# Attention with a long convolution on one core: the fill moves to 64x32 tiles, two results at a time, and PV of a new accumulator comes two turns late

## The chip, the cores and the metric

The kernel runs on one core of one Trainium2 chip. The metric is the device time of one execution in microseconds (us). Engines: PE is TensorE, DVE is VectorE, ACT is ScalarE, POOL is GpSimd, SP is SyncE.

## The reference

Two independent parts, put side by side in the last dimension of the output (2048 x 1024, f32). Part A is attention with 32 heads of 16 and one shared K and V; part B is a short and a long causal convolution with gates. Cut to what is computed:

```python
# A: x (1,2048,512), H = 32, Dh = 16
q = heads(x @ wq); k = x @ wk; v = x @ wv
p = softmax(einsum("bhqd,bkd->bhqk", q, k) * Dh**-0.5)
a = concat_heads(einsum("bhqk,bkd->bhqd", p, v)) @ wo
# B: q, k, v (1,2048,512)
k_shift = sum(k_pad[:, t:t+S, :] * shift_k[:, 3-t] for t in range(4))
kv = k_shift * v
y = irfft(rfft(kv, 4096) * rfft(ssm_k, 4096))[:, :2048] + kv * ssm_D
b = q * y
return concatenate([a, b], -1)
```

## The kernel before, in words

**The attention** (attend, L816) goes over 1024 tiles. A tile is one chunk of 128 keys (of 16) against 256 queries of each of four heads; 16 tiles share an accumulator, and two such groups make one of the 32 stacks n. For tile t, scores (L769) issues eight matmuls (S, L779), f16, 49 rows by 32 columns of PE, 512 columns wide: row half e of PE writes bank e of a two-bank tile s, of which there are two. One exponential on ACT (L787) reads both banks and writes p; seven p tiles rotate. pv (L790) issues eight f32 matmuls (P, L799; each runs as two passes, so the profile counts 16), 64 rows by 32 columns, 256 wide: row half e adds into the accumulator bank acc[e]. After 16 tiles DVE copies one accumulator and adds the other (L811, L812) and, but for the last two stacks, SP stores the sum to DRAM (L814).

The program uses eight banks of PSUM: four for s, and four (pool pf, L102, given out by bank) shared by the two accumulators and everything else on PE.

**Everything else is fill**, written as generators that yield before each piece of work: rest_of_q (L710: q of the other heads, then bounds for the exponent, L634), conv_pe (L432: transposes of the long kernel at L305; forward products with a table of cosines at L250 with a copy at L255; backward products at L397 with a multiplication by q at L426), conv_short and conv_dve (the element-wise work of the convolution on DVE), wo_heads and wo_part (L897: normalisation, then the output projection). Products run as mm (L200): four matmuls of 128 rows by 32 columns, side by side in column strips, so each product uses all 128 rows. f16 products are cut into hi and lo parts (three, L219). columns (L205) and products (L223) issue them in pieces: one result in one bank at a time, and a unit is 512 f16 or 128 f32 columns of one product.

**The order** is made ahead by _Fill (L983), as if two budgets ran along with the tiles. Every second tile, turn (L1018) adds RATE (L49) to them: 1.8 units of PE work and 1700 ns of DVE work, capped by MOST; threads other than the hurried one and conv_pe get at most EASY = 2 units. step (L1022) asks the threads in turn. A thread that has begun a result is the holder until it has finished it, and nobody else begins one. A yield of WAIT, n puts the thread off by n steps of two tiles. In attend the scores of tile x + 2 come first, then fill that goes on, P of tile x, and fill that is new; at the first tile of a group fill stands ahead of P. hurry (L703) lets q go first within LEAD steps of its need.

A prologue loads, transposes x and makes the first q; last (L957) ends the attention and the projection. The program has a second path for inputs of unusual size (_general), which is not taken here.

Of the kernel before, what the change touches and what calls it, by code (L numbers as in the profile page):

```python
# [48 lines left out]
RATE = 1.8, 1700.0  # L49
EASY = 2  # L50
MOST = 3.0, 2900.0
# [5 lines left out]
LEAD = 32  # L57
# [35 lines left out]
WHOLE, PARTS = 0, 1  # L93


class _Emit:
    def __init__(self, ctx, tc, I, out):
        self.ctx, self.tc, self.nc, self.I, self.out = ctx, tc, tc.nc, I, out
        e = ctx.enter_context
        self.c = e(tc.tile_pool(name="c", bufs=1))  # L100
        self.ps = e(tc.tile_pool(name="ps", bufs=2, space=PSUM))
        self.pf = e(tc.tile_pool(name="pf", bufs=4, space=PSUM))  # L102
        self.w = e(tc.tile_pool(name="w", bufs=2))
        self.dr = e(tc.tile_pool(name="dr", bufs=1, space=DRAM))
        self.n = 0
        self.step = 0
        self.seen = set()
# [97 lines left out]
    def columns(self, bank, first, w, x, last=False, dve=0):  # L205

        n, k = 0, x.shape[-1] // P
        while n < k:  # L210
            g = yield k - n, dve, CONT if bank else NEW, PARTS
            start = not bank
            if start:
                bank.append(self.bank())
            c = slice(P * n, P * (n + g))
            n += g
            self.mm(bank[0][:, P * first + c.start : P * first + c.stop], w, x[:, c], start, last and n == k)

    def three(self, w, x):  # L219

        return [(w[:, i], x[:, j]) for i, j in ((0, 0), (1, 0), (0, 1))]

    def products(self, bank, pairs, last=False, dve=0):  # L223

        n, k = 0, len(pairs)
        while n < k:
            g = yield k - n, dve, CONT if bank else NEW, PARTS
            start = not bank
            if start:
                bank.append(self.bank())  # L230
            for w, x in pairs[n : n + g]:
                n += 1
                self.mm(bank[0], w, x, start, last and n == k)
                start = False
# [15 lines left out]
    def forward(self, src, c, m, ft):  # L250

        b = []
        for q in range(2):
            yield from self.columns(b, 2 * q, ft[:, q, :], src, q == 1, 700 * q)
        self.nc.vector.tensor_copy(c[:, :, m, :], b[0].rearrange("p (q n) -> p q n", q=2))  # L255
# [9 lines left out]
    def conv_load(self):  # L265
# [3 lines left out]
        sk = self.w.tile([P, 4, 4], F32, tag="gn", bufs=2, name="sk")  # L269
        nc.sync.dma_start(sk, I["B_shift_k"].rearrange("(c p) t -> p c t", p=P))  # L270
        yield WAIT, 6
        yield 1, 600, NEW, WHOLE
# [19 lines left out]
    def long_forward(self, blk, hin, ch):  # L292
# [16 lines left out]
        for m in (0, 2):  # L309
            yield 2, 700, NEW, WHOLE  # L310
            turn(m)
        for m in range(0, 16, 2):
            if m < 12:
                ft[m // 2 + 2] = self.table("ff", m // 2 + 2)
                yield 2, 700, NEW, WHOLE
                turn(m + 4)
            for i in range(2):
                yield from self.forward(hT[m][:, i, :], ch, m + i, ft[m // 2][:, i])
# [51 lines left out]
    def short_forward(self, blk, cx):  # L370

        ft = {i: self.table("ff", i) for i in range(2)}
        for m2 in range(8):
# [3 lines left out]
            for i in range(2):  # L377
                yield from self.forward(self.kv2[m2][:, i, :], cx, 2 * m2 + i, ft[m2][:, i])
# [18 lines left out]
    def backward(self, blk, cx, places):  # L397
# [15 lines left out]
        for m2 in range(8):  # L413
# [5 lines left out]
            b = []  # L419
            for i in range(2):  # L420
                m = 2 * m2 + i
                for cc in range(2):
                    x = cx[:, cc, 4 * g2[m // 4] + g1[m % 4], :]
                    last = i == cc == 1
                    yield from self.columns(b, 2 * i, ft[m2][:, i, cc, :], x, last, 700 * last)
            nc.vector.tensor_tensor(r, b[0].rearrange("p (i n) -> p i n", i=2), q[m2], ALU.mult)  # L426
# [61 lines left out]
    def load(self):  # L488
# [4 lines left out]
        wkv = w.tile([P, 4, 32], F32, tag="gn", bufs=2, name="wkvf")  # L493
# [79 lines left out]
    def k_rows(self, c, cut):  # L573

        nc = self.nc
        h16 = self.w.tile([P, 512], F16, tag="gn", bufs=2, name=self.nm("kh"))
# [34 lines left out]
    def q_mm(self, g, c, b, dk):  # L611
        for i, (w, x) in enumerate(self.three(self.wq[g][:, :, dk, :], self.xT[c][:, :, dk, :])):
            self.mm(b, w, x, start=dk == i == 0, stop=dk == 3 and i == 2)

    def q_out(self, g, c, b, spread=False):
# [5 lines left out]
        qa = w.tile([P, 512], BF16, tag="qa", bufs=1, name=self.nm("qa"))  # L621
# [12 lines left out]
    def bound(self, g, c, b, st=None):  # L634
# [4 lines left out]
        gn = w.tile([8, 512], F16, tag="gn", bufs=2, name=self.nm("gn"))  # L639
# [70 lines left out]
    def rest_of_q(self):  # L710
# [5 lines left out]
        for c in range(4):  # L716
            for g in range(4):
                self.qn = c, g
                if c == g == 0:
                    continue  # L720
                if c or g > 1:
                    b = []
                    for dk in range(4):
                        pairs = self.three(self.wq[g][:, :, dk, :], self.xT[c][:, :, dk, :])
                        yield from self.products(b, pairs, dk == 3, 2600 * (dk == 3))
                    self.q_out(g, c, b[0])
                yield WAIT, 2
                yield 2, 1100, NEW, WHOLE
                self.bound(g, c, self.bank())
                self.qs.add((g, c))  # L730
# [20 lines left out]
    def flag(self):  # L751
# [10 lines left out]
        yield 1, 200, NEW, WHOLE  # L762
# [5 lines left out]

    def scores(self, u):  # L769


        n, (h, k) = u // (2 * NKT), divmod(u % (2 * NKT), NKT)
        if n >= NQ:
            return
# [15 lines left out]
    def pv(self, x):  # L790

        nc, w = self.nc, self.w
        n, (h, k) = x // (2 * NKT), divmod(x % (2 * NKT), NKT)
        if k == 0:
            self.acc = [self.bank() for _ in range(2)]
# [10 lines left out]
        if k < NKT - 1:  # L806
            return
        if h == 0:
            self.ao = w.tile([P, 512], F32, tag="ao", bufs=1, name=self.nm("ao"))
        cols = slice(256 * h, 256 * h + 256)  # L810
        nc.vector.tensor_copy(self.ao[:, cols], self.acc[0][:, 0:256])  # L811
        nc.vector.tensor_tensor(self.ao[:, cols], self.ao[:, cols], self.acc[1][:, 0:256], ALU.add)  # L812
        if n < NQ - 2:
            nc.sync.dma_start(self.od[n, :, cols], self.ao[:, cols])  # L814

    def attend(self, fill):  # L816
        self.od = self.dr.tile([NQ, P, 512], F32, name="od")
        tiles = 2 * NQ * NKT
        for x in range(tiles - 2):
# [66 lines left out]
    def wo_rows(self, i, groups):  # L886

        b = []
        for G in groups:
            yield from self.wo_row(b, i, G, G == groups[-1])  # L890
        return b[0]

    def wo_row(self, b, i, G, last):
        pairs = self.three(self.oc[G][:, :, i * P : (i + 1) * P], self.wo[G % 4])
        yield from self.products(b, pairs, last, 700 * last)

    def wo_part(self):  # L897
        nc, w, I = self.nc, self.w, self.I
        xr = self.out.rearrange("b (c p i) d -> (b c) p i d", c=4, p=P, i=4)
        for c in range(3):  # L900
            yield from self.after(("oc", 4 * c + 3))
            for i in range(4):
                b = yield from self.wo_rows(i, range(4 * c, 4 * c + 4))
                t = self.s2("wp", (512,))
                nc.vector.tensor_scalar(t, b, 1 / (OS * WS), None, ALU.mult)
                nc.sync.dma_start(xr[c][:, i, 0:D], t)
# [4 lines left out]
        for i in range(4):  # L911
            b = yield from self.wo_rows(i, range(12, 14))
            nc.vector.tensor_scalar(self.wp[i], b, 1 / (OS * WS), None, ALU.mult)
# [10 lines left out]
        for i in range(4):  # L924
            b = []
            yield from self.wo_row(b, i, 14, True)
            nc.vector.scalar_tensor_tensor(self.wp[i], b[0], 1 / (OS * WS), self.wp[i], ALU.mult, ALU.add)
        both = w.tile([P, 2, 4, 512], F32, tag="in", bufs=1, name="lr")
        t, self.lr = both[:, 0], both[:, 1]
        for h in range(2):  # L930
            while self.step < NKT * (NQ - 1) + 1 - NKT // 2 * (1 - h):
                yield WAIT, 1
            yield 0, 1800
            self.over(self.ao[:, 256 * h : 256 * h + 256], t, h)
        for i in range(4):
            b = []
            yield from self.columns(b, 0, t[:, 2, i * P : (i + 1) * P], self.wl[0], True, 700)
            nc.vector.tensor_tensor(self.wp[i], self.wp[i], b[0], ALU.add)
        while self.step < NKT * (NQ - 1) + NKT // 2 + 1:
# [43 lines left out]
class _Fill:  # L983
# [3 lines left out]
    def __init__(self, threads, hurry):  # L987
# [3 lines left out]
        self.used = 0  # L991
        self.holder = None

# [7 lines left out]
    def ask(self, t, i):  # L1001

        while t[0] is not None and t[2] <= i:
            if t[1] is None:
                self.go(t, None)
            elif t[1][0] == WAIT:
                t[2] = i + t[1][1]
# [5 lines left out]
    def give(self, t, n):  # L1013
# [4 lines left out]
    def turn(self):  # L1018
        self.used = 0
        self.credit = [min(c + r, m) for c, r, m in zip(self.credit, RATE, MOST)]  # L1020

    def step(self, i, new):  # L1022

        c, once = self.credit, True
        used = self.used
        more = True
        while more:
            more = False
            first = self.hurry()
            for t in sorted(self.threads, key=lambda t: t is not self.threads[first or 0]):  # L1030
# [4 lines left out]
                if a[0] > 0:  # L1035
                    most = int(c[0])
                    if t is not self.threads[1] and t is not self.threads[first or 0]:
                        most = min(most, EASY - used)
                    n = a[0] if a[3] == WHOLE else min(a[0], most)
                    if n < 1 or n > most or not (once and new or self.holder is t) or self.holder not in (None, t):  # L1040
                        continue
                    once = False
                elif c[1] <= 0 or not new:
# [4 lines left out]
                self.give(t, n)  # L1048
                more = True
                break  # L1050
        self.used = used
# [161 lines left out]
```

## Time and profile before

| what | value |
|---|---|
| median of 3 runs | 1091.48 us (1091.24 to 1093.11) |
| the profiled execution's own time | 1091.16 us |
| its span, first to last instruction | 1089.4 us |
| PE busy | 96% of the span |
| ACT busy | 91% |
| DVE busy | 63% |
| POOL busy | 10% |
| DMA queues q1 and q0, share of 16 engines | 12.6% and 11.6% |
| granted TensorE clock | 0.995 |

How to read it: a group's row names line, engine, operation, output <- input and shape, then busy time, mean ns of one, and the idle time of the engine just before, with what ended it. "128*32" or "64*32" behind a matmul is the part of PE that it uses, rows by columns. PEld is the weight load, which may overlap the matmuls. Matmuls are pipelined, so their starts say more than their ends. A row of the timeline gives start, length and count of merged instructions, in us from the start of the span.

### The profile page before, as it was taken

The numbers are of one execution on the slowest core, as the hardware profiler recorded it, in microseconds if no ns is written. First come the engines' busy times: TensorE is split into PE (matmuls) and PEld (weight loads), VectorE is DVE, ScalarE is ACT, GpSimd is POOL, SyncE is SP. The second block draws the span as 40 slices with busy tenths as digits, with TensorE's granted clock in tenths as the row PEclk, the third lists the DMA queues.
The fourth block names the chain that finished last, engine by engine and source line by source line (L and its number), as shares of the span: only waits on it lengthen the run. The fifth ranks groups of instructions, "written<-read, shape, count | busy, mean of one in ns | idle before, by whom it ended". The sixth has DMA issues, their size and how long they took to land.

```text
span 1089.4 us, 61326 instructions
## 1 busy us (share of the span) xinstructions
PE 1046.7 (96%) x28603; PEld 510.3 (47%) x28603; DVE 683.9 (63%) x978; ACT 988.3 (91%) x1038; POOL 105.3 (10%) x158
## 2 busy tenths in 40 slices
PE   6899999999999999999999999999999999999996
PEld 4344444445444444544454444444444445554432
DVE  3748676885178888884886467698889832121132
ACT  3699999999999999999999989999999999999974
POOL 3232101000000000013021311000000001210000
PEclk9999999999999999999999999999999999999999
DMA  7354614111322112114133532011131013221101
GB/s 232 114 149 163 197 50 145 52 51 49 113 70 86 31 35 64 55 59 137 40 116 100 177 108 99 30 46 45 60 98 51 30 35 109 87 79 31 36 3 43
DMA packets 51984, 89.18 MB, mean 82 GB/s; under 512 B 11612, under 2 KB 34186, under 8 KB 50700
## 3 DMA queue, kind: packets, MB, share of 16 engines
q1 hardware_dynamic: 38316, 43.50, 12.6%
q0 software_dynamic: 11648, 40.89, 11.6%
q8 instruction: 225, 3.69, 1.4%
q10 hardware_dynamic: 1760, 0.81, 0.3%
q14 instruction: 35, 0.29, 0.1%
HBM read 60.16 MB, written 25.02 MB: 78 GB/s over the span
## 4 chain that ended last, share of the span: by engine, by line
PE 76%; ACT 15%; issue 4%; DVE 3%; DMA 1%; ACTq 0%; SPq 0%; DVEq 0%
PE f L799 37%; PE s L779 19%; PE f L203 18%; ACT p L787 15%; PE f L305 1%; DVE xT L540 1%; DMA wqf<-in_A_wq 1%; PE f L638 0%; PE x L528 0%; ACT xT L539 0%; DMA qd<-gn 0%; PE x L203 0%; DVE t L362 0%; DVE ao L811 0%; DVE sp L255 0%
## 5 line engine op out<-in xcount | busy, mean ns | idle before, releaser
L787 ACT ACTIVATE p<-s 128x1024 f32<-128x1024 f32 x1024 | 976.6, 1039 | 70.4 <-PE s L779 41.2
L799 PE MATMUL f<-p,vx 64*32 64x256 f32 x16384 | 667.6, 381 | 3.6 <-DVE ao L811 2.0
L779 PE MATMUL s<-st,kst 49*32 49x512 f16 x8192 | 436.0, 381 | 14.4 <-issue 4.3
L799 PEld LDWEIGHTS f<-p,vx 64*32 64x32 f32 x16384 | 277.0, 106 | 182.8 <-issue 99.6
L779 PEld LDWEIGHTS <-kst 49*32 49x32 f16 x8192 | 164.9, 90 | 177.2 <-issue 114.4
L141 DVE TENSOR_TENSOR sp<-sp 128x1024 f32<-128x1024 f32 x96 | 111.7, 1212 | 0.0
L255 DVE COPY sp<-f 128x512 f32<-128x512 f32 x64 | 44.1, 689 | 89.5 <-PE f L203 89.3
L811 DVE COPY ao<-f 128x256 f32<-128x256 f32 x64 | 27.0, 421 | 99.9 <-PE f L799 99.8
L203 PE MATMUL f<-xT,wq 128*32 128x512 f16 x768 | 61.8, 395 | 0.0
L203 PE MATMUL f<-wo,o 128*32 128x512 f16 x720 | 59.1, 385 | 0.7 <-issue 0.7
L141 DVE TENSOR_TENSOR sp<-sp,sp 128x1024 f32<-128x1024 f32 x48 | 56.6, 1217 | 0.3
L203 PE MATMUL f<-a,ff 128*32 128x128 f32 (+1 forms) x792 | 45.4, 314 | 0.4 <-issue 0.4
L259 POOL DMA_DIRECT2D ff<-in_ff x32 | 17.5, 549 | 288.0 <-PE f L203 288.0
L203 PE MATMUL f<-sp,fi 128*32 128x128 f32 (+1 forms) x784 | 43.6, 315 | 0.0
L203 PE MATMUL f<-hT,ff 128*32 128x256 f32 (+1 forms) x632 | 42.8, 350 | 0.0
L426 DVE TENSOR_TENSOR r<-f,q 128x512 f32<-128x512 f32 x16 | 11.0, 690 | 48.6 <-PE f L203 48.6
L427 POOL DMA_DIRECT2D out<-r x16 | 11.4, 714 | 238.7 <-DVE r L426 224.7
L364 DVE TENSOR_TENSOR a<-a,t 128x512 f32<-128x512 f32 x48 | 33.1, 690 | 1.3
L362 DVE TENSOR_TENSOR t<-kk,tpb 128x512 f32<-128x512 f32 x48 | 32.8, 683 | 0.0
L203 PEld LDWEIGHTS <-wq 128*32 128x32 f16 x768 | 14.2, 96 | 39.6 <-issue 38.2
L203 PEld LDWEIGHTS f<-a,ff 128*32 128x32 f32 x792 | 16.8, 108 | 33.0 <-issue 28.8
L812 DVE TENSOR_TENSOR ao<-ao,f 128x256 f32<-128x256 f32 x64 | 27.0, 421 | 7.7 <-DVE ao L811 0.9
(136 smaller groups left out, 576.8 us busy)
## 6 DMA issues: line engine op xcount, KB each, us to landing
ff<-in_ff POOLq DMA_DIRECT2D x32, 256.0 KB, 4.7
od<-ao SPq DMA_DIRECT2D x60, 128.0 KB
kk<-in_B_k POOLq DMA_DIRECT2D x12, 640.0 KB, 5.4
qd<-qp SPq DMA_DIRECT2D x48, 128.0 KB
st<-qd SPq DMA_DIRECT2D x60, 98.0 KB
v<-in_B_v POOLq DMA_DIRECT2D x16, 256.0 KB, 5.9
hin<-in_B_ssm_k POOLq DMA_DIRECT2D x4, 1024.0 KB, 6.8
fi<-in_fi POOLq DMA_DIRECT2D x16, 256.0 KB, 3.9
```

The source lines that it names most:

```text
L141: v.tensor_tensor(part(out), part(a), part(b), op)
L203: self.nc.tensor.matmul(out[j : j + 32], w[:, j : j + 32], x, start=start, stop=stop)
L255: self.nc.vector.tensor_copy(c[:, :, m, :], b[0].rearrange("p (q n) -> p q n", q=2))
L259: self.nc.gpsimd.dma_start(t, self.I[n][:, 2 * m2 : 2 * m2 + 2])
L362: nc.vector.tensor_tensor(t, kx(i), tap(i), ALU.mult)
L364: nc.vector.tensor_tensor(a, a, t, ALU.add)
L427: nc.gpsimd.dma_start(self.orr[:, 2 * m2 : 2 * m2 + 2, D + blk * CB : D + (blk + 1) * CB], r)
L779: self.nc.tensor.matmul(s[j : j + 32, e, :], self.kst[rows, k * P + j : k * P + j + 32], self.st[n][rows, :, 256 * h : 256 * h + 256], sta ...
L787: self.nc.scalar.activation(p, s, AF.Exp, scale=DH**-0.5 / SC / SC)
L799: nc.tensor.matmul(self.acc[e][32 * j : 32 * j + 32, 0:256], self.vx[rows, k, :], self.pt[x][rows, j % 2, 256 * (j // 2) : 256 * (j // 2) ...
L811: nc.vector.tensor_copy(self.ao[:, cols], self.acc[0][:, 0:256])
L812: nc.vector.tensor_tensor(self.ao[:, cols], self.ao[:, cols], self.acc[1][:, 0:256], ALU.add)
```

## The change

- Fill is issued by halves, which takes two results a and b of the same number of products and two banks. In the first half, row half 0 of PE works for a in bank 0 and row half 1 for b in bank 1, each on its own 64 rows of the contraction; then the thread waits (WAIT 1.5), and in the second half the row halves change places: row half 0 now adds to b's bank and row half 1 to a's. Each matmul has 64 rows by 32 columns. forward, backward, rest_of_q and wo_part now make two results at a time; backward's multiplication is split by result. Transposes and bounds stay as they were.
- _Fill has one call per tile, after P: 1.15 units and 850 ns per tile, at most EASY = 2 units a tile for all threads, caps 4 units and 1700 ns. WAIT counts tiles, twice the number given. After a result is done, no thread begins another for GAP = 2 tiles. LEAD is 44.
- plan puts P of tiles 0 and 1 of a group at tile 2's turn and P of tiles 2 and 3 at tile 3's.
- qa shares the buffers "gn", of which there are three instead of two; ao of the last stack uses buffer "r".

```diff
-RATE = 1.8, 1700.0
+RATE = 1.15, 850.0
 EASY = 2
-MOST = 3.0, 2900.0
+MOST = 4.0, 1700.0
-LEAD = 32
+LEAD = 44
+GAP = 2
...
+    def halves(self, a, b, grain, dve=0):
+        banks = []
+        for half in range(2):
+            n, k = 0, len(a)
+            while n < k:
+                g = yield (k - n) * grain, dve * half, CONT if banks else NEW, grain
+                start = not banks
+                if start:
+                    banks += [self.bank(), self.bank()]
+                for m in range(n, n + g // grain):
+                    for e in range(2):
+                        out, (cols, w, x) = banks[half ^ e], (a, b)[half ^ e][m]
+                        r = slice(64 * e, 64 * e + 64)
+                        for j in range(0, P, 32):
+                            self.nc.tensor.matmul(
+                                out[j : j + 32, cols],
+                                w[r, j : j + 32],
+                                x[r],
+                                start=half == m == 0,
+                                stop=half == 1 and m == k - 1,
+                            )
+                n += g // grain
+            if half == 0:
+                yield WAIT, 1.5, CONT
+        return banks
...
     def forward(self, src, c, m, ft):
-        b = []
-        for q in range(2):
-            yield from self.columns(b, 2 * q, ft[:, q, :], src, q == 1, 700 * q)
-        self.nc.vector.tensor_copy(c[:, :, m, :], b[0].rearrange("p (q n) -> p q n", q=2))
+        work = [[(slice(CB * q, CB * q + CB), ft[:, i, q, :], src[:, i, :]) for q in range(2)] for i in range(2)]
+        b = yield from self.halves(*work, 2, 1400)
+        for i in range(2):
+            self.nc.vector.tensor_copy(c[:, :, m + i, :], b[i].rearrange("p (q n) -> p q n", q=2))
...
+            b = yield from self.halves(*work, 2, 850)
+            for i in range(2):
+                nc.vector.tensor_tensor(r[:, i, :], b[i][:, cols], q[m2][:, i, :], ALU.mult)
...
+                    b = yield from self.halves(*work, 1, 5200)
+                    for i in range(2):
+                        self.q_out(g + i, c, b[i])
...
+    def plan(self):
+        plan = {}
+        for x in range(2 * NQ * NKT):
+            plan.setdefault(x + {0: 2, 1: 1, 2: 1}.get(x % NKT, 0), []).append(x)
+        return plan
...
             self.scores(t)
-            self.step = x // 2
-            if x % 2 == 0:
-                fill.turn()
-            if x % NKT == 0:
-                fill.step(self.step, True)
-                self.pv(x)
-            elif x % 2:
-                self.pv(x)
-            else:
-                fill.step(self.step, False)
-                self.pv(x)
-                fill.step(self.step, True)
+            self.step, self.slot = x // 2, x
+            for y in plan.get(x, []):
+                self.pv(y)
+            fill.turn(x)
...
             if self.holder is None:
+                self.free = i + GAP
...
+                    most = min(int(c[0]), EASY - used)
+                    n = min(a[0], most) // a[3] * a[3]
+                    if n < 1 or self.holder not in (None, t) or (self.holder is None and i < self.free):
                         continue
```

More of the change, by code (lines that the diff above doesn't have):

```diff
@@ L203, in mm @@
             self.nc.tensor.matmul(out[j : j + 32], w[:, j : j + 32], x, start=start, stop=stop)
[L205 to L217, printed above, removed]
[L219 to L234 removed]
+    def halves(self, a, b, grain, dve=0):
[23 more added lines that the diff above has]
+        return banks
+    def three(self, w, x):
+        return [(slice(0, 512), w[:, i], x[:, j]) for i, j in ((0, 0), (1, 0), (0, 1))]
     def parts(self, engine, hi, lo, x, scale):
@@ L884, in wo_heads, with wo_rows @@
             self.seen.add(("oc", G))
[L886 to L895, printed above, removed]
+    def wo_rows(self, i, groups, dve):
+        work = [
+            [y for G in groups for y in self.three(self.oc[G][:, :, r * P : (r + 1) * P], self.wo[G % 4])] for r in (i, i + 1)
+        ]
+        return (yield from self.halves(*work, 1, dve))
     def wo_part(self):
```

159 lines of the change are left out of this document (77 added, 82 removed).

## The prediction

> **What bounds the kernel now.** I read the page first: who is busy, and what the chain that ended last is made of.
>
> ```profile
> PE 1046.7 (96%) x28603; PEld 510.3 (47%) x28603; DVE 683.9 (63%) x978; ACT 988.3 (91%) x1038; POOL 105.3 (10%) x158
> ...
> PE 76%; ACT 15%; issue 4%; DVE 3%; DMA 1%; ACTq 0%; SPq 0%; DVEq 0%
> ...
> L787 ACT ACTIVATE p<-s 128x1024 f32<-128x1024 f32 x1024 | 976.6, 1039 | 70.4 <-PE s L779 41.2
> ```
>
> PE carries the chain, yet ACT is nearly as busy: 1024 exponentials, one per tile of the attention. How fast would each go alone? The timeline of a stretch without any fill, 815 to 840 us, tells it:
>
> ```profile
> 814.25 26.77 ACT L787 ACTIVATE p<-s 128x1024 f32<-128x1024 f32 x29
> ...
> 815.40 0.41 PE L779 MATMUL s<-st,kst 49*32 49x512 f16 x8
> ...
> 815.62 0.63 PE L799 MATMUL f<-p,vx 64*32 64x256 f32 x16
> ...
> 816.31 0.41 PE L779 MATMUL s<-st,kst 49*32 49x512 f16 x8
> ```
>
> 29 exponentials without a gap in 26.77 us; less the length of the last one (1.02) that is 25.75 / 28 = **0.92 us a tile: ACT's pace**. PE starts scores (S) every 0.92 us and PV (P) 0.22 behind, then stands. The next view is the timeline of a stretch with fill (the backward products), where PE never stands:
>
> ```profile
> 960.33 0.64 PE L799 MATMUL f<-p,vx 64*32 64x256 f32 x16
> ...
> 960.76 0.42 PE L779 MATMUL s<-st,kst 49*32 49x512 f16 x8
> ...
> 961.11 0.16 PEld L203 LDWEIGHTS f<-sp,fi 128*32 128x32 f32 x8 [0.38 <-issue]
> 961.11 0.43 PE L203 MATMUL f<-sp,fi 128*32 128x128 f32 x8
> ...
> 961.47 0.66 PE L799 MATMUL f<-p,vx 64*32 64x256 f32 x16
> ...
> 962.63 0.41 PE L779 MATMUL s<-st,kst 49*32 49x512 f16 x8
> ...
> 962.97 0.64 PE L203 MATMUL f<-sp,fi 128*32 128x128 f32 x16
> ...
> 963.55 0.66 PE L799 MATMUL f<-p,vx 64*32 64x256 f32 x16
> ```
>
> Starts are what counts, since ends are modelled. P to S is 0.43 (960.33 to 960.76), S to P 0.22, so a tile of attention costs PE 0.65. The first visit to the fill has one unit (8 rows: 128 columns of f32, two passes, four column strips; half of the P that takes 0.43, so 0.21): S to P grows from 0.22 to 0.71, by 0.49. The second has two units: 0.92, grown by 0.70, of which the work is 0.43. **Each visit costs 0.28 us beside its work.** S and P also change shape and type, but not tile, 64 rows by 32 columns, and pay nothing. How many visits are there? The waits of the weight loads count them, with three other waits that I need below:
>
> ```profile
> PEld f L203 <- issue: 89.8, 230, 2.8
> DVE sp L255 <- PE f L203: 89.3, 42, 5.0
> PEld L203 <- issue: 78.4, 217, 1.0
> ...
> PEld f L799 <- DVE ao L811: 19.5, 48, 1.0
> ```
>
> 230 + 217 = 447 visits, 447 x 0.28 = 125 us of PE. And here is the stretch in which the exponentials run:
>
> ```profile
> L787 ACT ACTIVATE p<-s x1024: 1017/1023/1248, 35.7 to 1074.1; 128x1024 f32<-128x1024 f32 x171
> ```
>
> 1074.1 - 35.7 = 1038.4 us for 1024 tiles; at 0.92 it would be 942. The 96 us between them are all that the change can touch. The 35.7 ahead and the 15.3 behind (1089.4 - 1074.1) stay, as do the 1.8 outside the span (1091.16 - 1089.4); the profiled execution is 0.3 under the median, 1091.48.
>
> **The change part by part.**
>
> Fill on 64x32 tiles (halves): two results of k products are k steps of eight matmuls, twice over. A step is the shape of S (f16, 512 columns, 0.22) or of P (f32, 256 columns, 0.43), and a pair takes the same units of 0.21 as its two results took. Work is unchanged, so what goes is 0.28 for each of 447 visits. The 16 transposes (L305) and some 15 bounds (L638) keep other tiles:
>
> ```profile
> 200.33 0.62 PE L799 MATMUL f<-p,vx 64*32 64x256 f32 x16
> 200.88 0.53 PEld L305 LDWEIGHTS f<-ident,hin 128*128 128x128 f32 x4 [0.41 <-issue]
> ...
> 201.53 0.41 PE L779 MATMUL s<-st,kst 49*32 49x512 f16 x8
> ```
>
> P to S is 1.20 here, 0.77 more than 0.43.
>
> PE's work is then 1024 x 0.65 = 666 and about 170 of fill, below 942: ACT is next late, and what is left are turns in which PE is late for it. How late may it be? The scores of tile t have to wait until the exponential of t-2 has left its bank. After that one's end the next is busy for another 0.92 - 0.10 = 0.82 (1.02 long, 0.92 apart), and from S to ACT there go:
>
> ```profile
> 966.31 0.41 PE L779 MATMUL s<-st,kst 49*32 49x512 f16 x8
> ...
> 966.85 1.02 ACT L787 ACTIVATE p<-s 128x1024 f32<-128x1024 f32 x1 [0.38 <-PE s L779]
> ```
>
> 0.54. With 0.05 for the hand-over, an estimate, 0.23 is the slack: lateness beyond it stalls ACT.
>
> Budget. 1.15 units a turn and at most two (EASY): a conv pair of 8 units takes turns 2, 2, then a wait of int(2 x 1.5) = 3 turns, again 2, 2, then GAP: the pattern 2,2,0,0,2,2,0. A turn of two is 0.65 + 0.43 = 1.08, 0.16 over the pace; two of them 0.32, stall 0.09, and the empty turns make it up. 67 pairs (32 forward, 16 backward, 7 of q, 12 of wo) x 2 x 0.09 = **12**. A transpose turn is 0.65 + 0.77 = 1.42: 0.50 - 0.23 = 0.27, x16 = **4**. The bounds' turns stay within the slack. MOST and LEAD only move fill earlier.
>
> PV two turns late (plan): of a group of 16 tiles, turns 0 and 1 have no P, turns 2 and 3 have two: 0.22 + 2 x 0.43 = 1.08 each. Without fill that is the stall of 0.09. With two units in one of them 0.52, in both 0.95; sliding the pattern along gives both in 2 of 7 places, one in 4, none in 1: (2 x 0.95 + 4 x 0.52 + 0.09) / 7 = 0.58, less 0.10 that such turns cost anyway. Some 800 units at 1.14 a turn fill 70% of 1022 turns, 45 of 64 groups: 45 x 0.48 + 19 x 0.09 = **23**; from below 6 (0.09 each), from above 61 (0.95 each). What it buys, the end of the 19.5 us of waits of P for ao's addition, is in the 96 already.
>
> Two banks. Fill has two of the four, so a pair waits for the copies of the one before:
>
> ```profile
> 965.01 0.43 PE L203 MATMUL f<-sp,fi 128*32 128x128 f32 x8
> ...
> 965.50 0.69 DVE L426 TENSOR_TENSOR r<-f,q 128x512 f32<-128x512 f32 x1 [1.73 <-PE f L203]
> ```
>
> ```profile
> L141 DVE TENSOR_TENSOR sp<-sp 128x1024 f32<-128x1024 f32 x96 | 111.7, 1212 | 0.0
> L255 DVE COPY sp<-f 128x512 f32<-128x512 f32 x64 | 44.1, 689 | 89.5 <-PE f L203 89.3
> ...
> L812 DVE TENSOR_TENSOR ao<-ao,f 128x256 f32<-128x256 f32 x64 | 27.0, 421 | 7.7 <-DVE ao L811 0.9 <-PE f L305 0.5
> ...
> L619 DVE TENSOR_SCALAR cut<-f 128x512 f32<-128x512 f32 x16 | 11.0, 689 | 20.7 <-PE f L203 20.5
> ...
> L628 DVE TENSOR_TENSOR qp<-cut,qp 128x512 f16<-128x512 f32 x15 | 10.4, 693 | 0.5
> ...
> L629 DVE SCALAR_TENSOR_TENSOR qa<-cut 128x512 bf16<-128x512 f32 x15 | 10.3, 685 | 0.0
> ...
> L627 DVE CAST qp<-cut 128x512 f16<-128x512 f32 x15 | 6.4, 427 | 0.6
> ```
>
> A copy starts 0.28 after the fill has streamed (965.01 + 0.21 to 965.50); two forward copies end at 0.28 + 2 x 0.69 = 1.66. GAP puts the next pair two turns on, at 0.65 + 0.65 = 1.30 (PE late) to 0.92 + 0.65 = 1.57 (PE on time): it waits 0.1 to 0.36, and behind it on PE the next S. I take 0.25 for 16 long pairs and 12 of wo, 7 us. Short pairs start when eight DVE products are through, later than that, and backward's two multiplies are 128x256 now, 0.42 each (as L812): 1.12, hidden, for 0.15 more of DVE. For q the second bank is read after 0.28 + 0.69 + 0.43 + 0.69 + 0.69 + 0.69 = 3.5: a conv pair of another thread may wait up to 2.1; I take 1.0, 7 us. Together **14**, between 0 and 28 x 0.36 + 7 x 2.1 = 25 as long as DVE is on time.
>
> DMAs: the same number and sizes. q's six stores stand in a row on SP now instead of three; the loads of stacked q behind them are issued 20 turns (18 us) ahead of need. Buffers of gn: a third one, shared with qa, so nothing waits anew. More matmul instructions (f16 fill eight a unit instead of four): nothing, or one more stall such as the chain has:
>
> ```profile
> 50.61 2.63 issue
> ```
>
> Start and end keep stalls; in these windows ACT is busy for 19.9 and 19.6 of 25:
>
> ```profile
> 40.00:65.00 25.00, 19.94 (x22) 0.93 0.42 136
> ...
> 1040.00:1065.00 25.00, 19.63 (x21) 0.93 0.01 3
> ```
>
> **10**, as before. Sum: 942 + 10 + 12 + 4 + 23 + 14 = 1005; + 35.7 + 15.3 + 1.8 = **1058 us**, 3% less.
>
> **The rivals.**
>
> R1, the fill hides: pairs seldom fall on turns 2 and 3, and a wait for copies falls on turns 0 and 1, where PE has 0.7 to spare. Then 942 + 10 + 12 + 4 + 6 = 974: **1027 us** and below, to 1005 with the fixed 63 alone. For it: PE has 100 us of room. Against: at 1.14 units a turn no stretch of conv is free of such turns.
>
> R2, DVE takes PE's place: with two banks each pair waits for DVE, and if DVE is one L141 operation (1.21) behind whenever a pair ends, 67 x 1.21 = 81 more: **1139 us**, slower. It decides from (1091 - 1058) / 67 = 0.5 us more wait a pair. Against: DVE was the one that waited at 42 of 64 forward copies. For: there were two banks in reserve, so that lateness cost nothing, and the same DVE credit a turn (850, before 1700 in two) comes 3% faster. The Trainium skill (TensorEngine Tiling (Array Packing), PSUM Bottleneck) warns that tiling speeds up TensorE and not the emptying of PSUM, which may become the bound; that is this rival, and the 42 of 64 speak against it so far.
>
> R3, the change doesn't do what it says: the 0.28 is the price of entering any other stream, such as weights that could not be loaded ahead (0.38 to 0.41 ahead of the first load, above). Pairs spread 800 units over some 470 visits: conv's two-unit turns become 1.36, each 0.44 over, two in a row stall 0.65 instead of 0.09; 96 such bursts (48 pairs x 2) x 0.56 = 54, and in the 45 late groups 8 of 7 x 0.28 = 0.32 each, 14, wo's and q's one-unit turns (0.65 + 0.28 + 0.21 = 1.14, some 250, 0.22 each) 55: 1058 + 123 = **1181 us**. Against: S and P alternate at no price. The Trainium skill (the same page, Key Properties) says that a change of mode drains TensorE and a change of tile doesn't; by that R3 can't be.
>
> **How the numbers follow.** Forecast 0.55 (1027 to 1096), R1 0.18, R2 0.17, R3 0.07, and 0.03 for stalls that just eat up the gain. Within 0.2%, about what a measurement of this kernel tells from no change, is 1089 to 1094. Faster: 0.54 of the forecast, 0.18 and the weak end of R2, 0.03: 0.75; same 0.04; slower 0.21. The range, 1015 to 1115, leaves out the lower third of R1, most of R2 and R3; the forecast's own bounds are 1058 - 17 - 14 (late PV at its 6, no wait for copies) and 1058 + 38 (late PV at its 61).
>
> **What would show it.** Right: fill matmuls as 64*32, no 0.28 around them, S every 0.92 to 1.1 with fill, ACT's stretch near 1005. Late PV: longer intervals of ACT at tiles 4 to 6 of each 16. Two banks: PE waiting for L255, cut or wp. R2 has these waits above 50 us; R3 keeps 0.2 us of "issue" at each visit. The forecast falls if PE stands still for another reason, or if ACT's pace itself changes.

## The result, and the profile after

The change makes the kernel **slower by 0.35%**: 1096.2 us (median of 19 runs, 1089.88 to 1102.16) against 1091.92 (19 runs, 1088.97 to 1095.33), ratio 1.0035, interval 1.0021 to 1.0049. The forecast was 1058. The profiled execution of after, 1102.16, is the longest of its 19, 6 us over the median; its span is 1100.4.

From the page of after: the busy shares, the chain that ended last, and the exponentials.

```profile
PE 988.4 (90%) x30907; PEld 597.8 (54%) x30907; DVE 681.7 (62%) x994; ACT 979.9 (89%) x1038; POOL 104.6 (10%) x158
...
ACT 45%; PE 36%; issue 11%; DVE 7%; DMA 1%; ACTq 0%; SPq 0%; DVEq 0%
...
L789 ACT ACTIVATE p<-s 128x1024 f32<-128x1024 f32 x1024 | 968.1, 1050 | 86.0 <-PE s L781 78.3
```

PE lost its place on the chain as foreseen, 76% to 36%, and ACT took it, 15% to 45%. But "issue" grew from 4% to 11%, and ACT stands idle for 86.0 us where it stood for 70.4. The exponentials as a group of the tile p, with the first and the last start:

```profile
L789 ACT ACTIVATE p<-s x1024: 1014/1032/1202, 37.6 to 1083.1; 128x1024 f32<-128x1024 f32 x171
```

1083.1 - 37.6 = 1045.5 us; before it was 1038.4, and the forecast had 1005. Was the price of a visit not removed? The timeline of after around a visit of q's products says it was:

```profile
86.67 0.56 PE L781 MATMUL s<-st,kst 49*32 49x512 f16 x8
86.88 0.78 PE L801 MATMUL f<-p,vx 64*32 64x256 f32 x16
...
87.31 0.78 PE L221 MATMUL f<-xT,wq 64*32 64x512 f16 x16
...
87.75 0.57 PE L781 MATMUL s<-st,kst 49*32 49x512 f16 x8
...
87.96 0.61 PE L801 MATMUL f<-p,vx 64*32 64x256 f32 x4
...
91.18 0.67 PE L801 MATMUL f<-p,vx 64*32 64x256 f32 x6 [2.61 <-issue]
```

P at 86.88, two units of fill at 87.31, S at 87.75: 0.43 + 0.44, the bare work, and not 0.28 more. The same rows show what took its place. After four of P's sixteen matmuls PE stops, at 88.20 by the records one by one, and goes on at 91.18: 2.98 us in which it waits for nothing that the profile can name. The chain of after has six pieces of "issue" of over 2 us. That of before had two, the one that the prediction quoted and one near the end:

```profile
1047.63 2.32 issue
```

In after:

```profile
51.98 2.12 issue
88.57 2.61 issue
...
142.26 2.26 issue
199.81 2.55 issue
...
594.56 3.20 issue
...
1057.38 2.24 issue
```

The last piece of each is of another kind: the product behind it reads lr, which DVE finishes just ahead of it (at 1059.41 in after, where PE goes on at 1059.59). So five pieces stand against one.

Where did ACT's time go altogether? I took the 1023 intervals between starts of exponentials, less 0.9155 each (the median where no fill runs), and put each one over by 0.04 down to the longest stand of PE shortly before its S: to issue, to a wait for DVE or DMA, or, if PE only stood for ACT or not at all, to PE's own work being too long. This is my own sum over the trace, and puts down a turn that is late because of an earlier stall to PE's work; how far back a stand of PE is looked for moves a few us between the columns. In us, of the profiled executions (those of after and spread_skip_most2 are the longest of their runs, each some 6 us over its median):

| kernel | profiled time | lost | PE's own work | issue | DVE, DMA |
|---|---|---|---|---|---|
| before | 1091.2 | 102 | 84 | 12 | 7 |
| after | 1102.2 | 109 | 66 | 36 | 12 |
| rows128 | 1144.4 | 154 | 143 | 14 | 0 |
| before_late | 1126.3 | 134 | 125 | 11 | 1 |
| pv_now | 1107.0 | 116 | 56 | 40 | 23 |
| less_dma | 1083.8 | 92 | 65 | 17 | 16 |
| more_dma | 1120.9 | 130 | 73 | 49 | 11 |
| spread_skip_most2 | 1089.4 | 93 | 51 | 29 | 17 |
| ssm2_less | 1068.4 | 72 | 45 | 18 | 13 |

(The parts sum to a few us more than the loss, since intervals below 0.9155 + 0.04 sum to -1 to -5.) From before to after PE's own work gave back 18 us only, and issue took 24.

**What the issue stalls are.** A second one, in the timeline around 200 us, cuts an S in two after three of its eight matmuls:

```profile
199.42 0.39 PE L781 MATMUL s<-st,kst 49*32 49x512 f16 x3
...
202.36 0.10 PEld L781 LDWEIGHTS <-kst 49*32 49x32 f16 x5 [2.85 <-issue]
202.36 0.40 PE L781 MATMUL s<-st,kst 49*32 49x512 f16 x5 [2.55 <-issue]
```

No operand is missing halfway through one group, so it is the instructions that are late. The page has a queue for them; its row in before, and then in after:

```profile
q8 instruction: 225, 3.69, 1.4%
```

```profile
q8 instruction: 243, 3.98, 1.5%
```

3.69 MB in 225 packets and 3.98 MB in 243 are 16,384 bytes each. PE has 57,206 instructions before (28,603 matmuls and as many weight loads) and 61,814 after, and its sequencer 77 and 79 more (semaphores, nearly all): divided by 256 that is 223.8 and 241.8, so there is one packet for every 256 instructions of PE, and one over. In after 16 issue stalls of 0.8 us and more, from start to start, lie between the first and the last exponential (7 in before). Counted in PE's instructions modulo 256, those of the sequencer included, 15 of the 16 stand at exactly one place, 193, and so do 6 of the 7; anywhere-in-the-block stalls would be spread over 0 to 255. The one left over in each kernel is the wait for lr. At all 15 PE goes on 2.2 to 2.7 us after the start of a packet on this queue (for 91.18, the packet of 88.61). **So PE stood at the end of one block of 256 instructions, waiting for the next.** The packets there come 5 to 8 us apart, where the median is 4.1; at full pace PE uses a block up in 3.4 us (16 instructions in the 0.215 us of S). The Trainium skill (Runtime: NRT & Kernel Launch, Instruction fetch mechanics) has the block, 16 KiB or 256 instructions, and says that the fetch is mostly hidden; the size agrees with these rows, and most blocks here pass without a stall, but at these 15 places the fetch isn't hidden.

Why late? The windows of after around two stalls and, last, one without fill; the last two columns are the busy share of the 16 DMA engines and GB/s:

```profile
86.00:91.00 5.00, 2.57 (x80) 1.60 (x65) 1.29 (x2) 3.44 (x4) 1.63 (x3) 0.96 1.05 266
...
197.00:202.00 5.00, 2.73 (x83) 1.54 (x70) 1.80 (x3) 2.96 (x3) 0.00 (x0) 1.00 0.99 379
...
700.00:705.00 5.00, 3.84 (x120) 2.03 (x127) 4.90 (x7) 5.00 (x6) 0.00 (x0) 1.00 0.04 14
```

Data transfers fill the engines (1.05, 0.99) when PE stands; over the whole stretch of the exponentials the share is 0.25. Counted over all 239 blocks of after between the exponentials: the packet of the next block starts a median 0.9 us after PE has entered a block, but 2.3 to 5.0 us after it ahead of the 15 stalls, and the packet itself takes no longer there (0.9 to 1.2 us) than elsewhere (0.9 to 1.8). In 28 blocks, all with fill, data kept the engines' busy share at 0.6 or more over the first 2 us: there the packet starts a median 2.5 us in, and 14 of the 15 stalls end such a block. Of the 164 other blocks with fill, which PE uses up as fast (3.8 us against 4.0), one ends in a stall. Before had 21 blocks with such data and its packets were as late there (2.2 us), but PE took 4.5 us for a block: 6 stalls. What holds the packet back, the engines themselves or the memory behind them, these rows don't tell apart. My theory: the blocks queue behind data, and a PE that works faster through more instructions asks for them sooner. The rival: the transfers matter only through what DVE and PE wait for, and the gain was eaten by the late P and the bursts.

**The late P.** The timeline of after at the turns of positions 2 and 3 of a group:

```profile
451.26 1.06 PE L801 MATMUL f<-p,vx 64*32 64x256 f32 x32
452.13 0.63 PE L221 MATMUL f<-hT,ff 64*32 64x256 f32 x16
...
452.56 0.41 PE L781 MATMUL s<-st,kst 49*32 49x512 f16 x8
...
452.78 1.06 PE L801 MATMUL f<-p,vx 64*32 64x256 f32 x32
453.10 1.02 ACT L789 ACTIVATE p<-s 128x1024 f32<-128x1024 f32 x1 [0.26 <-PE s L781]
453.64 0.63 PE L221 MATMUL f<-hT,ff 64*32 64x256 f32 x16
...
454.07 0.41 PE L781 MATMUL s<-st,kst 49*32 49x512 f16 x8
...
454.62 1.94 ACT L789 ACTIVATE p<-s 128x1024 f32<-128x1024 f32 x2 [0.49 <-PE s L781]
```

Two P (0.87) and two units (0.43) make S come 1.51 apart twice; ACT stands 0.26 and 0.49. In the sum above, 33 of PE's 66 us fall on tiles 5 and 6 of the groups, which are these turns (a turn issues the S of two tiles on, and the next S is the late one).

### The profile page after: what moved, and what is told of

Its sections match the earlier page's. It is cut to its first block, busy times and chain, and to the rows that moved or that the text cites. A ratio compares the mean times of both kernels' runs of the same rounds, so it can differ in the third digit from the quotient of the medians.

```text
span 1100.4 us, 65958 instructions
## 1 busy us (share of the span) xinstructions
PE 988.4 (90%) x30907; PEld 597.8 (54%) x30907; DVE 681.7 (62%) x994; ACT 979.9 (89%) x1038; POOL 104.6 (10%) x158
## 3 DMA queue, kind: packets, MB, share of 16 engines
q8 instruction: 243, 3.98, 1.5%
## 4 chain that ended last, share of the span: by engine, by line
ACT 45%; PE 36%; issue 11%; DVE 7%; DMA 1%; ACTq 0%; SPq 0%; DVEq 0%
ACT p L789 44%; PE f L801 16%; PE s L781 9%; PE f L221 9%; PE f L306 1%; DVE sp L142 1%; PE f L204 1%; DMA wqf<-in_A_wq 1%; DVE xT L540 1%; DVE gm L651 1%; DVE cut L619 0%; PE x L528 0%; DVE sp L256 0%; DVE gn L640 0%; PE x L204 0%
## 5 line engine op out<-in xcount | busy, mean ns | idle before, releaser
L781 PE MATMUL s<-st,kst 49*32 49x512 f16 x8192 | 474.3, 383 | 64.0 <-ACT p L789 36.8
L801 PEld LDWEIGHTS f<-p,vx 64*32 64x32 f32 x16384 | 343.8, 107 | 111.9 <-issue 23.7
L221 PE MATMUL f<-xT,wq 64*32 64x512 f16 x1344 | 69.5, 379 | 3.6 <-issue 2.1
L221 PE MATMUL f<-wo,o 64*32 64x512 f16 x1440 | 71.7, 376 | 1.2 <-DVE cut L619 0.8
L221 PE MATMUL f<-a,ff 64*32 64x256 f32 x1024 | 54.1, 383 | 4.1 <-DVE cut L619 2.1
L221 PE MATMUL f<-hT,ff 64*32 64x256 f32 x1024 | 46.5, 376 | 1.9 <-issue 1.8
L221 PE MATMUL f<-sp,fi 64*32 64x256 f32 x1024 | 46.1, 376 | 0.0
L221 PEld LDWEIGHTS <-o 64*32 64x32 f16 x1440 | 27.6, 92 | 15.4 <-issue 3.7
L221 PEld LDWEIGHTS <-wq 64*32 64x32 f16 x1344 | 26.2, 93 | 17.7 <-issue 4.5
L221 PEld LDWEIGHTS f<-a,ff 64*32 64x32 f32 x1024 | 24.8, 106 | 17.1 <-issue 3.3
```

What stands on the lines that cost most here:

```text
L221: self.nc.tensor.matmul(out[j : j + 32, cols], w[r, j : j + 32], x[r], start=half == m == 0, stop=half == 1 and m == k - 1,)
L781: self.nc.tensor.matmul(s[j : j + 32, e, :], self.kst[rows, k * P + j : k * P + j + 32], self.st[n][rows, :, 256 * h : 256 * h + 256], sta ...
L801: nc.tensor.matmul(self.acc[e][32 * j : 32 * j + 32, 0:256], self.vx[rows, k, :], self.pt[x][rows, j % 2, 256 * (j // 2) : 256 * (j // 2) ...
```

## The experiments

Ratios are to the kernel before, run on the same chip, with their intervals.

**rows128**: the visits paid for again, all else as after. halves issues its steps as whole 128x32 products:

```diff
-                    for e in range(2):
-                        out, (cols, w, x) = banks[half ^ e], (a, b)[half ^ e][m]
...
+                    cols, w, x = (a, b)[half][m]
+                    self.mm(banks[half][:, cols], w, x, m == 0, m == k - 1)
```

> The changed kernel with its own plan, banks and order, but the fill's products on 128 rows by 32 columns again: the first half makes result a whole, the second result b. Theory 1 (the price of a visit, 0.28 us, is a price of changing the tile, and the change did remove it): some 500 visits get it back, turns of two units go from 1.08 to 1.36 us, and the time goes from 1096 to 1180 to 1220 us. Rival (entering any other stream costs this, or nothing was removed): 1096 within 4 us.

1148.3, ratio 1.0509 (1.0461 to 1.0557). Between the two expectations: in one and the same plan the price of the visits is worth 52 us (1148.3 - 1096.2), not 125. From S to S with two units of fill between it takes 1.32 to 1.34 us there (medians by kind of fill, 222 turns) and 1.08 in after: about 0.25 a visit. The 52 are a net figure, since in the table PE's own work grows by 77 and the two columns behind it fall by 34. R3 is out: there is a price, and the change removed it. rows128 has 55,830 instructions on PE, 10% fewer than after, at the slower pace, and the waits of PE put down to issue are

```profile
PE f L792 <- issue: 4.5, 5, 1.2
...
PE f L204 <- issue: 2.5, 3, 1.5
PE s L772 <- issue: 2.0, 1, 2.0
```

9.0 us in all, where after has 24.8:

```profile
PE f L801 <- issue: 12.7, 11, 3.2
...
PE f L221 <- issue: 7.1, 5, 2.2
...
PE s L781 <- issue: 5.0, 4, 2.5
```

**pv_now** issues each P in its own turn (`plan.setdefault(x, []).append(x)`).

> The changed kernel with every PV at its own turn. Theory 1 (two PVs in one turn make PE late: 33 us of ACT's lost time of the changed kernel stand at the tiles 5 and 6 of the groups, where other tiles lose about 2.4 us each): 28 us go and at most some 10 us of waits for the old accumulator's copies come: 1073 to 1083 us. Rival (with two banks for the fill the delay is needed: 64 waits of about 0.9 us, of which 0.4 is beyond the slack): 1094 us or more.

1107.55, 1.0129 (1.0077 to 1.018): the rival. The late P, which I had counted as a cost, saves 11 us in the new plan. Its trace says how: tiles 5 and 6 lose 31 us less than in after, but tile 3, whose S stands behind the first P of a new accumulator, loses 34 us where it lost none; that P now waits for DVE's copies of the old one (28 us of waits of its weight loads).

**before_late** gives the kernel before the same late P, at its old places between the fill.

> The kernel before, with nothing changed but the PV plan of the changed kernel (two turns late for the first PV of a group, two PVs in turns 2 and 3). Theory 1 (late PVs cost where fill stands in the same turns): turn 2 becomes 1.08 + 0.28 + 0.38 = 1.74 us, some 0.5 us more lost in each of about 50 groups, less 6 us of waits for the accumulator: 1105 to 1117 us. Rival (PE has room for it): 1085 to 1092 us.

1125.91, 1.0294 (1.0245 to 1.0343): worse than both. With the visits still at 0.28, two P and a visit in one turn lose 34 us; 38 of PE's 125 fall on tile 5 of the groups alone.

**less_dma** lightens the loads of after: one DFT table of each kind is loaded once and used for all, the rolling windows of k stop at the third, and v isn't loaded (a slice of k's window stands in for it), so that 22.8 of 60.2 MB are not read; all other work stays. **before_less_dma** is the same in the kernel before.

```diff
-        t = self.w.tile([P, 2, 2, P], F32, tag="ft", bufs=FT, name=self.nm(n))
-        self.nc.gpsimd.dma_start(t, self.I[n][:, 2 * m2 : 2 * m2 + 2])
-        return t
+        if n not in self.tab:
...
+        return self.tab[n]
...
-            if m2 + 2 < 8:
+            if m2 + 2 < 3:
```

> The changed kernel without most of the loads of the short convolution and of the tables: one table of each kind and three windows of k are loaded and used again, v isn't loaded (the k window stands in its place). PE, ACT and DVE do the same work. Theory 1 (PE waits for its own instructions, a block of 256 at a time, when data transfers fill the DMA engines: 36 us of ACT's lost time in the changed kernel, 12 in the one before): these waits fall below 12 us and the time to 1068 to 1076 us. Rival (the waits come from PE's denser stream alone, or from something that the profile doesn't show): 1096 within 4 us.

> The kernel before without most of the loads of the short convolution and of the tables, as in the changed kernel's run without them (one table of each kind and three windows of k used again, no v). Theory 1 (instruction blocks come late where data fills the DMA engines, and PE before used its instructions slower, so it seldom ran dry: 12 us of ACT's lost time, of which some 5 at the start stay): 4 to 7 us go, 1085 to 1088 us. Rival (less data helps in some other way, such as loads that arrive sooner): as much as in the changed kernel, 14 us, 1078 us.

1081.9, 0.989 (0.9844 to 0.9935), and 1088.76, 0.9969 (0.9946 to 0.9992). The same transfers cost after 14 us and before 3 (1088.76 is just over the range expected). In after the long issue stalls fall from 16 to 5, and the waits to

```profile
PE f L222 <- issue: 5.1, 4, 2.2
...
PE f L802 <- issue: 3.0, 3, 2.6
...
PE s L782 <- issue: 2.8, 5, 2.0
```

while those for DVE and DMA don't fall (12 to 16 in the table). That speaks for the theory, by taking away; but the gain is 14 us where I had expected 20 to 28, and ACT still loses 17 us to issue, where I had expected less than 12.

**more_dma** goes the other way: after each table's load the same 256 KB are copied once more, into memory that nothing reads.

```diff
         self.nc.gpsimd.dma_start(t, self.I[n][:, 2 * m2 : 2 * m2 + 2])
+        d = self.dr.tile([P, 2, 2, P], F32, name=self.nm("dd"))
+        self.nc.gpsimd.dma_start(d, self.I[n][:, 2 * m2 : 2 * m2 + 2])
         return t
```

> The changed kernel, with every load of a DFT table (48 of 256 KB) followed by a second transfer of the same 256 KB into memory that nothing reads. Nothing on the cores waits for it. Theory: TensorE's instruction blocks come late when data transfers fill the DMA engines, so more transfers mean more late blocks: issue stalls of 0.8 us and more go from 15 to 20 or over, the waits put down to issue from 25 to 32 us or more, and the time up by 6 to 20 us, to 1102 to 1116. Rival: TensorE's stalls don't hang on the transfers, and the lighter loads helped only through DVE and the two banks: 1094 to 1099, stalls 13 to 17.

1119.58, 1.0229 (1.0197 to 1.026): 23 us over after, more than the theory's 20. The stalls of 0.8 us and more are 26, all at 193 modulo 256 but for the last, the wait for lr, and the waits are 37.8:

```profile
PE f L803 <- issue: 20.6, 17, 3.5
PE s L783 <- issue: 8.8, 7, 2.6
PE f L221 <- issue: 8.4, 7, 2.2
```

No operation on the cores depends on these copies, and the DVE and DMA waits stay (11). The rival falls. Of the 21 us that ACT loses over after, 13 are issue and 7 PE's own work.

The next kernels try to smooth PE's work. **skip** forbids fill in turns 2 and 3 of a group, where two P stand:

```diff
-            fill.turn(x)
+            fill.turn(x, x % NKT in (2, 3))
...
-                    most = min(int(c[0]), EASY - used)
+                    most = 0 if rest else min(int(c[0]), EASY - used)
```

> The changed kernel, but no fill products in the two turns of a group that carry two PVs (turns 2 and 3); the credit is kept for later turns. Theory 1 (late PVs cost because the fill stands beside them: tiles 5 and 6 lose 33 us): these fall to 0.1 us a group, about 6 us, and the time to 1068 to 1076 us. Rival (two PVs in a turn cost by themselves, or PE's room elsewhere is too small to take the fill that is pushed out): 1090 us or more.

1096.82, 1.0042 (1.0012 to 1.0072): the rival, nothing gained. Tiles 5 and 6 lose 14 instead of 33, but the fill kept back follows in rows of two-unit turns and the loss turns up elsewhere (PE's own work 65 to 72 and issue 38 to 45, by how far back a stand of PE is looked for).

**spread_skip** has P of positions 0 to 3 two turns late and of 4 to 8 one, so that two P stand in turns 5 and 9, apart, and forbids fill there.

> The changed kernel with the late PVs made up one by one: PVs 0 to 3 of a group come two turns late, 4 to 8 one turn, so that turns 5 and 9 carry two PVs, and these two take no fill. Theory 1: a turn of 1.08 us alone is 0.16 over the pace and within the slack of 0.23, so late PVs cost nothing: 1064 to 1074 us, a little under the run that only keeps the fill out of turns 2 and 3. Rival (PVs that stay late hold buffers of p or delay the accumulator): 1085 us or more.

1100.09, 1.0074 (1.0044 to 1.0104), a miss, in the rival's range: PE's own work 64, issue 35.

**most2** lets unused credit pile up to 2 units, not 4 (`MOST = 2.0, 1700.0`), so that kept-back fill is not caught up in long rows.

> The changed kernel with the PE credit capped at 2 units instead of 4, so that no two turns of two units follow each other. Theory 1 (such bursts cost 0.09 to 0.2 us each, and with the late PVs' neighbours make the 33 us that ACT loses outside tiles 5 and 6): 10 to 20 us go, 1076 to 1086 us. Rival (fill now takes more turns, so more groups have it beside their late PVs, and what is saved is given back): 1092 to 1100 us.

1090.87, 0.9992 (0.9963 to 1.0021): between the two expectations, 5 us under after, PE's own work 56. **r100m2** and **r90m3** lower RATE too (1.0 with MOST 2; 0.9 with MOST 3), for fewer two-unit turns.

> The changed kernel with 1.0 unit a tile instead of 1.15 and the credit capped at 2 instead of 4; all else as changed. Theory 2 (with 1.15 units PE has 0.65 + 1.15 x 0.21 = 0.89 us of work a tile against ACT's 0.92, so no lateness is made up, while 128 tiles later on have no fill at all; spread thinner, the same fill costs less): the first 640 tiles run at 1.00 instead of 1.06 us, the idle stretch shrinks, and the time is 1080 to 1087 us. Rival (the fill's stalls are per pair, whatever the rate, and the convolution only gets later): 1090 us or more.

> The changed kernel with 0.9 units a tile, the rate of the kernel before, and the credit capped at 3, its cap before. Theory 2: as with 1.0 and 2, a little more of the idle stretch is used, but credits of 3 allow two turns of two units in a row again: 1080 to 1090 us. Rival (stalls are per pair, whatever the rate): 1094 us or more.

1095.1, 1.0026 (1.0 to 1.0051), and 1094.11, 1.0017 (0.9992 to 1.0042), both in the rival's range. A lower rate brings nothing.

**spread_skip_most2** joins the two, **spread_most2** leaves out the skip, and **most2_less** and **ssm2_less** put the lighter loads of less_dma under most2 and spread_skip_most2.

> P of positions 0 to 3 two turns late and of 4 to 8 one turn late, so that no turn but those of positions 5 and 9 has two, no fill in these two, and MOST 2, so that the fill left out isn't caught up in long rows of two-unit turns. Theory: the late P and the bursts are the remaining cost, 1065 to 1078. Rival: PE's busy time beyond the pace only moves to other turns and the waits for instruction blocks stay, as with the earlier two that left out fill in chosen turns: 1088 to 1100.

> As spread_skip_most2, but fill is allowed in the turns of positions 5 and 9. It tells what of the 12.5 us under the changed kernel comes from leaving fill out of the turns with two P and what from spreading the late P with MOST 2. Theory: a turn with two P and two units of fill costs 0.5 us, and with two such turns in each group instead of two in a row a part of that stays: 1086 to 1091. Rival: spreading alone does it: 1081 to 1085.

> MOST 2 and the lighter loads of less_dma together (one table of each kind, three windows, no v: the output is then not the reference's). Theory: what the instruction blocks wait for behind data transfers and what the bursts of fill cost are separate sums, so the gains add: 14 us of less_dma and 1 us of MOST 2 under the changed kernel, about 1077 (1073 to 1082). PE's issue stalls of 0.8 us and more are then 8 or fewer. Rival: the issue stalls only show where PE would have been late anyway; smoothing the fill as well then brings back nothing, or the fill that comes later meets another wait: 1082 to 1090.

> The plan of spread_skip_most2 (1083.7) with the lighter loads of less_dma (the output is then not the reference's). Theory: the waits behind transfers are a sum of their own, 14 to 16 us as under the changed kernel and under MOST 2: 1066 to 1071. Rival: this plan has hidden part of them already: 1075 to 1083.

spread_skip_most2: **1083.74, 0.9913 (0.9889 to 0.9937)**, with the whole computation; it beats both kernels, by 8 and 12 us, and lies between the two expectations. ACT runs through a piece of q's fill without an idle gap that the view shows, two P included:

```profile
429.12 31.15 ACT L789 ACTIVATE p<-s 128x1024 f32<-128x1024 f32 x33
...
443.68 1.09 PE L801 MATMUL f<-p,vx 64*32 64x256 f32 x32
```

spread_most2: 1094.24, 1.0007 (0.9985 to 1.0029), over both expectations; so with P spread the skip is worth 10.5 us once MOST is 2, and MOST 2 is worth 16 once there is a skip (1100.09 to 1083.74), while each alone gave 5 or less. most2_less: 1075.51, 0.9831 (0.9804 to 0.9859), as the theory had it: 15 us under most2. ssm2_less: 1065.05, 0.9724 (0.9688 to 0.976), 19 us under spread_skip_most2 and just under the range expected. The loads' cost adds to that of the plan and isn't hidden by a better one.

## Why the prediction was wrong

**Right: the price of a visit exists and goes.** The weight loads' waits that counted 447 visits are now

```profile
PEld L221 <- issue: 8.1, 12, 2.6
...
PEld f L221 <- issue: 7.7, 10, 2.7
```

22 times, and P, two units and S stand 0.87 apart. Also right: ACT takes over the chain; the fill's own time; that the waits for the two banks are small: 14 was forecast, and all that ACT loses to DVE and DMA is 12 (7 in before). R2 would have needed over 50 us of such waits; it falls. Of the 0.28 x 447 = 125 us, which the sum never booked as a gain (it starts from ACT's pace), rows128 shows that 52 net lie on the path. In the kernel before a turn with one unit was hidden under ACT's pace (S to S 1.14, but the turn behind it 0.73: no time lost on ACT, medians of 86), and only those with two units paid (a median of 0.19 lost each, with the turn behind; 322 such turns, some 60 us, and more where a turn visited the fill twice).

**Wrong, and the largest single step: "More matmul instructions: nothing, or one more stall such as the chain has."** The prediction had the stall's row, 2.63 us of issue, in its hands, and booked it with the fixed 10 at start and end. Issue cost ACT 12 us in before and 36 in after, 24 more (in profiled executions, of which that of after is a long one); less_dma and more_dma show that the transfers set it, and rows128 that fewer instructions at a slower pace meet less of it (14). The argument that PE has 100 us of room hides the point: while PE catches up it runs at its full pace, and a block is then used up in 3.4 us. The 0.9 us until the next packet starts, as a median, and the 2.2 to 2.7 us from there to the restart leave next to nothing of that.

**Too small: the late P, 23.** Tiles 5 and 6 lose 33, within the bounds of 6 and 61. In groups where PE has no other stand the two turns together lose a median of 0.28 us without fill (25 groups; 0.09 forecast), 0.57 to 0.59 with two units in one of them (11 groups; 0.52) and 0.99 with two in both (7 groups; 0.95): it is the price without fill that was too low. That it is a cost at all has to be read beside pv_now: without it the kernel is 11 us slower. The prediction had what it buys as "in the 96 already"; at tile 3 it is 34 us of the new plan.

**Too small: the bursts, 12.** A two-unit turn behind another one stalls 0.165 (80 undisturbed turns) instead of 0.09, the first 0.036 instead of 0 (78 turns): 16 us. Credit up to 4 units makes longer rows than the pattern 2,2,0,0,2,2,0; with MOST 2 it is 5 us less.

Together, in the terms of the sum: PE's own work 39 forecast (12 + 4 + 23), 66 measured; fixed stalls 10, issue 36; two banks 14, all waits for DVE and DMA 12. 63 became 109 (114 less 5 for the short intervals). The pace gives back 5 (936.6 for 942), so the stretch is 40.5 us longer than the 1005, as measured; 2 us each are added ahead of it (37.6 for 35.7) and behind it. R1 falls with the same rows. Of the 27 us by which PE's own work is over its forecast, 10 are the late P and some 4 the bursts; what of the other 13 are longer rows of fill and what turns still late behind an issue stall, one trace can't part, and it stays open.

## What to carry to other kernels

A price per visit is worth only what lies beyond the pace of the engine that is next late: pay it back in one and the same plan (rows128) before counting calls. When an engine gets faster, look at how often it needs new instructions, and what the DMA engines are doing just then; a piece of "issue" in the chain is a price with a rate, not a constant. Work that is kept back must not return in one row: leaving out fill under two P and capping the credit each gave 5 us or less, both together with the spread 12.

## What the runs showed of the hardware

TensorE's instructions come in packets of 16,384 bytes, one for every 256 instructions, on a DMA queue of their own. The packet of the next block starts a median 0.9 us after TensorE has entered a block, but 2.5 us where data keeps the busy share of the 16 DMA engines at 0.6 or more over the block's first 2 us; TensorE goes on 2.2 to 2.7 us after the packet's start and stands until then, for 0.8 to 3.6 us, in the middle of an operation if need be. That befell 14 of 28 such blocks where it used a block up in 4.0 us (after) and 6 of 21 where it took 4.5 (before). 48 copies of 256 KB that nothing waits for cost 23 us; leaving out 22.8 MB of reads gave 14 us back in the faster kernel and 3 in the slower. Products on 64x32 tiles go in between S and P at no price (0.43 for 16 matmuls of 512 columns in f16 or 256 in f32), where 128x32 products in the same plan cost about 0.25 a visit and the kernel 52 us more.
